# Two kinds of attention in one kernel: riding score units that may start later, and a new order from the 400th exponential on

## The chip, the core and the metric

The kernel runs on one core of a Trainium2 chip. The metric is the device time of one execution in microseconds (us), from its start to its last write. The core has a matrix engine (TensorE, PE in the profile), a vector engine (VectorE, DVE), an activation engine (ScalarE, ACT), a general engine (GpSimd, POOL) and a queue that issues most of the transfers (SyncE, SP). Matrix products land in PSUM, an accumulator memory whose banks hold 512 float32 columns on 128 partitions.

## The reference

One input x of 2048 tokens and 640 columns goes through two attentions with 32 heads of 20 columns each, and a gate mixes them:

```python
x = A_x
g = _sigmoid((x * gate_w).sum(-1, keepdims=True))
a = _A_ref(x, A_wqkv, A_wo)      # softmax over all 2048 keys
b = _B_ref(x, B_wqkv, B_wo)      # softmax over 8 keys: pos, pos-2, ..., pos-14
return g * a + (1 - g) * b
```

Attention A is the large part: 32 heads, 2048 queries and 2048 keys make 134 million exponentials. Attention B (window 8, step 2) is small in arithmetic, but has its own projections, and its elementwise products run on VectorE.

## The kernel before

**Groups, units, tiles.** Attention A is cut into 32 groups (GROUPS, L34): four heads times 512 queries. A group has 64 units: one head of the four, one block of 128 keys, 512 queries, so a unit is one score matmul with a 128x512 result. Two or three units make a tile; its scores lie side by side in PSUM, and one ACTIVATE with Exp on ScalarE (`exp`, L2000) turns a tile into bf16 in `ebuf`. Then matmuls (`pv`, L2045) multiply them with V and accumulate the whole group in one bank, `obank`. When a group is complete, `gen_norm` divides by the sums (which come out of the same matmuls, from a column of ones), multiplies by the gate and puts the result into `oTd`.

**Riding units.** A unit need not go through ScalarE. VectorE can make an approximation of the exponential: `clamp` (L1958) adds an offset to the scores and writes them as int16 into `uD`, whose bits are then read as bf16. Four such units, the four heads of one key block, make a quad. The quad enters the sum as four slices: `uD` itself and three copies with shifted exponents (`eD`), made either by one VectorE instruction for up to four units (`gen_d`, L1058) or in pieces of one unit on GpSimd (`piece`, L1089). Each slice has its own weight in V (`vS`, made on GpSimd, L1108). So a quad takes four units from ScalarE, and gives VectorE and GpSimd four clamps and three copies, and TensorE three slices of four matmuls more than the one set it would have had anyway. A riding unit's score matmul is issued together with a tile's ("rides" on it) into the third PSUM bank of the tile or another free one; so a tile that carries one has two units of its own as a rule.

**Banks.** Three PSUM banks serve everything else (BANKS: bank 0 is `sbank`, banks 1 and 2 are the last thirds of the two score buffers): projections, attention B, output blocks, riding units, and third units of tiles. In the profile, products into bank 0 are named side, those into 1 and 2 score.

**The planner.** Nothing of the order is written out by hand. While the program is built, a planner (`_Sched`) keeps an estimated time for each engine, emits tile after tile, and between them runs side jobs (Python generators with priorities: attention B in `gen_bproj` and `gen_b`, norms, output blocks in `gen_fold`, the riding copies in `gen_d`). The chip then executes each engine's fixed list, and semaphores keep the dependencies. Which job comes when depends on 22 numbers, and the table PLAN gives new ones at certain tile numbers:

```python
(SLACK, XTOL, XPRIO, XLATE, DWAIT, DIDLE, DIDLE2, DTIME, DLOW, DLATE, DVE_AHEAD, DAHEAD, BOOST, XBOOST, RFILL,
 FILL, HOLD, BOFF, EVS, FRT, PTAPS, PLATE) = plan
```

Among them are DTIME (a quad may be opened only while the exponentials still to come last at least that many us by the planner's clock, test in `wanted`), DIDLE and DIDLE2 (how idle VectorE must be for a ride), PTAPS (how many of attention B's products go to GpSimd), and the priorities of the side jobs.

**The end.** The last 512 tokens' output needs attention A and B of all heads. `gen_prefold` computes the parts that are ready earlier and stores them; `gen_prefold2` accumulates output blocks 2 and 3 in banks 0 and 1 and leaves them there for `tail`; before it takes the bank for block 3 it waits for `d_over`. `crowded` keeps bank 1 free of third units once no more than TLAST = 14 units of the last group are left. `tail` adds the last group's share after its norm (`gen_norm_last`, L950 to L969), and sends the rows out.

Of the kernel before, what the change touches and what calls it, by code (L numbers as in the profile page):

```python
# [423 lines left out]
def _build(ctx, nc, A_x, A_wqkv, A_wo, B_wqkv, B_wo, gate_w, out):  # L424
# [1480 lines left out]
    def d_over():  # L1905

        lo, hi = ahead[NG - 1]
        return cur["g"] >= NG - 1 and (4 * hi - lo) * UNIT < DTIME and not dopen
# [370 lines left out]
```

## Time and profile before

| | us |
|---|---|
| median of three runs | 775.98 (775.81 to 776.1) |
| the profiled execution, as a run | 776.33 |
| its span, from the first to the last instruction | 774.4 |
| first exponential of a tile starts | 18.0 |
| exponentials begun by 439.19 | 400 |
| last exponential ends | 766.41 |

The profile is of one execution. Its span leaves out what lies around the instructions, here 1.9 us. A row of a group gives the line, the engine, the operation, the tiles it writes and reads, the count, the union of the busy time and the mean duration of one, and the idle time of the engine before such instructions with what ended it. A row of a timeline gives the start, the length, and how many like instructions were merged. A row of windows gives the busy time of each engine in a stretch of the span. Instructions of one engine overlap at their ends in such records, so a sum of durations can exceed the union.

### The profile page before, as it was taken

To read this page: it belongs to the slowest core of one execution; us is meant where nothing else is said; L and a number is where in the kernel's file an instruction comes from. 1 tells how busy PE (TensorE), PEld (TensorE's weight loads), DVE (VectorE), ACT (ScalarE), POOL (GpSimd) and SP (SyncE) were. 2 spreads that over 40 slices of the span, in tenths; PEclk is the share of its full clock that TensorE was granted. 3 is DMA by queue.
4 is the path that set the end of the run, shared out by engine and by line. 5 is a ranking of instruction groups with operands and counts; after the bars stand their busy time and mean duration, and the time that the engine had idled before them with its cause. 6 is when DMAs were issued, how large, how long until landed. Compare 5 with 4: busy or idle time off the path is not lost.

```text
span 774.4 us, 30166 instructions
## 1 busy us (share of the span) xinstructions
PE 743.5 (96%) x12409; PEld 291.0 (38%) x12409; DVE 696.8 (90%) x1263; ACT 756.6 (98%) x747; POOL 353.8 (46%) x603
## 2 busy tenths in 40 slices
PE   8999999999998999999998999999999999999897
PEld 5433333332343343334334334433443423344233
DVE  6698978999999999979999999998999999998993
ACT  5999999999999999999999999999999999999996
POOL 4255633455753464344354445544453544253330
PEclk9999999999999999999999999999999999999999
DMA  7321122020111252331231122423204211133411
GB/s 232 113 64 38 31 61 60 26 47 14 40 36 36 54 130 67 80 98 52 74 95 45 24 57 61 96 65 91 49 27 110 52 27 49 46 71 82 109 31 37
DMA packets 71456, 49.89 MB, mean 64 GB/s; under 512 B 43096, under 2 KB 64872, under 8 KB 71320
## 3 DMA queue, kind: packets, MB, share of 16 engines
q1 hardware_dynamic: 70376, 47.54, 24.3%
q8 instruction: 99, 1.62, 0.9%
q10 hardware_dynamic: 944, 0.43, 0.2%
q14 instruction: 37, 0.30, 0.1%
HBM read 32.79 MB, written 7.62 MB: 52 GB/s over the span
## 4 chain that ended last, share of the span: by engine, by line
PE 45%; ACT 33%; issue 15%; DVE 6%; DMA 1%; SPq 0%; ACTq 0%; DVEq 0%
ACT ebuf L2000 33%; PE score L1981 14%; PE obank L2045 13%; PE side L691 11%; PE score L691 4%; DVE uD L1958 2%; DVE eD L1058 1%; DMA oB<-in_A_x_dram 1%; PE side L1239 1%; PE score L2066 0%; PE score L1685 0%; PE side L1347 0%; PE obank L2066 0%; DVE dst L841 0%; DVE kvw L1226 0%
## 5 line engine op out<-in xcount | busy, mean ns | idle before, releaser
L2000 ACT ACTIVATE ebuf<-score 128x1024 bf16<-128x1024 f32 (+1 forms) x706 | 743.2, 1198 | 3.0 <-PE score L1981 1.6
L1958 DVE TENSOR_SCALAR uD<-score 128x512 int16<-128x512 f32 x428 | 286.0, 681 | 30.0 <-PE score L1981 28.0
L1981 PE MATMUL score<-qT,kT 32*128 32x512 bf16 x1854 | 257.0, 384 | 16.5 <-ACT ebuf L2000 11.7
L1089 POOL TENSOR_TENSOR eD<-uD,two 128x256 int32<-128x256 int32 x311 | 186.7, 615 | 123.3 <-DVE eD L1058 59.3
L1058 DVE TENSOR_SCALAR eD<-uD 128x2048 int16<-128x2048 int16 (+3 forms) x295 | 173.6, 612 | 4.4 <-PE obank L2045 4.0
L2045 PE MATMUL obank<-ebuf,vA 128*21 128x512 bf16 x1616 | 152.7, 385 | 0.9 <-ACT ebuf L2000 0.7
L1981 PEld LDWEIGHTS score<-qT,kT 32*128 32x128 bf16 x1854 | 63.7, 91 | 211.4 <-ACT ebuf L2000 148.3
L1108 POOL TENSOR_TENSOR vS<-vA,vw 128x252 bf16<-128x252 bf16 x108 | 65.4, 606 | 111.7 <-DVE eD L1058 66.0
L2045 PE MATMUL obank<-eD,vS 128*21 128x512 bf16 x1296 | 110.7, 379 | 0.0
L691 PE MATMUL side<-xT,wBs 128*32 128x256 bf16 x2400 | 95.6, 281 | 0.7 <-DVE rQ L1301 0.5
L691 PEld LDWEIGHTS side<-xT,wBs 128*32 128x32 bf16 x2400 | 68.3, 141 | 28.6 <-issue 16.3
L1031 POOL TENSOR_TENSOR oN<-oTt,oN 128x256 bf16<-128x256 f32 x60 | 47.5, 791 | 58.7 <-DVE eD L1058 29.3
L2045 PEld LDWEIGHTS obank<-ebuf,vA 128*21 128x21 bf16 x1616 | 36.7, 89 | 82.8 <-issue 60.3
L1164 DVE CAST qkvB<-side 128x512 bf16<-128x512 f32 (+1 forms) x72 | 42.1, 594 | 3.9 <-PE side L691 3.6
L1335 DVE TENSOR_TENSOR kvw<-kvw,eB 128x2048 bf16<-128x2048 bf16 (+1 forms) x40 | 44.5, 1138 | 0.0
L1226 DVE TENSOR_TENSOR kvw<-qkvB 128x1792 bf16<-128x1792 bf16 (+2 forms) x40 | 44.4, 1133 | 0.1
L2045 PE MATMUL obank<-uD,vA 128*21 128x512 bf16 x432 | 41.9, 379 | 0.0
L2045 PEld LDWEIGHTS obank<-eD,vS 128*21 128x21 bf16 x1296 | 31.5, 91 | 19.6 <-issue 2.0
L1016 POOL TENSOR_TENSOR rcp<-rcp,gA 128x16 f32<-128x16 f32 x30 | 7.8, 259 | 56.2 <-DVE rcp L1012 26.8
L1981 PE MATMUL score<-woBp,kT 32*128 32x512 bf16 x188 | 30.0, 384 | 1.7 <-ACT ebuf L2000 0.9
L691 PE MATMUL side<-xT,kvw 128*32 128x512 bf16 (+1 forms) x340 | 28.6, 383 | 0.5 <-DVE vA L917 0.2
L691 PE MATMUL side<-kvw,xT 128*32 128x160 bf16 (+1 forms) x760 | 28.5, 262 | 0.5
(212 smaller groups left out, 575.5 us busy)
## 6 DMA issues: line engine op xcount, KB each, us to landing
kvw<-scr_v SPq DMA_DIRECT2D x32, 336.5 KB
oN<-scr_n SPq DMA_DIRECT2D x60, 128.0 KB
scr_v<-qkvB SPq DMA_DIRECT2D x32, 85.0 KB
wBs<-in_B_wqkv_dram SPq DMA_DIRECT2D x5, 480.0 KB
WqP<-in_A_wqkv_dram SPq DMA_DIRECT2D x14, 160.0 KB
oTd<-oN SPq DMA_DIRECT2D x108, 20.0 KB
out_dram<-outsb SPq DMA_DIRECT2D x12, 160.0 KB
qT<-dst SPq DMA_DIRECT2D x93, 20.0 KB
```

The lines of the kernel that those rows point to most:

```text
L691: ins = e.matmul(o[j:k, :], l(j) if callable(l) else l[:, j:k], r, start=(first and i == 0), stop=(last and i == n - 1), skip_group_check= ...
L1031: T("pool", 0.73, lambda e, cols=cols: e.tensor_tensor(oN[0][:, cols], oTt[:, cols], rcpR[:, cols], ALU.mult), reads=["oTt", "oN%d" % i], ...
L1058: T("dve", 0.065 + 0.1334 * (n - m), lambda e, k=k, sl=sl, m=m: e.tensor_scalar(eD[:, sl % NS, 512 * m:512 * n].bitcast(I16), uD[d % 2][:, ...
L1089: T("pool", PDUR, lambda e: e.tensor_tensor(eD[:, sl % NS, 512 * i:512 * (i + 1)].bitcast(I32), uD[d % 2][:, 512 * i:512 * (i + 1)].bitcas ...
L1108: T("pool", 0.607, lambda e: e.tensor_tensor(vS[:, d % 2, :, :], _ap(vA, (kb * NQ + q) * 4 * DV, [[0, K - 1], [1, 4 * DV]]), _ap(vw, 0, [[ ...
L1164: t = TB(dvc(n * TOK), lambda e, o=o, i=i: e.tensor_copy(o, i), reads=[("side", b)], writes=[key])
L1226: TB(dvc(n_ * TOK, 2), lambda e: e.tensor_tensor(o, i0, i1, ALU.mult), reads=["qB", "kB"], writes=prods(i, range(n_)) + olds(), port=True)
L1335: TB(dvc(n_ * 2 * TOK, 2), lambda e: e.tensor_tensor(o, i0, i1, ALU.mult), reads=rd, writes=prods(i, range(2 * n_)), port=True)
L1958: t = T("dve", 0.598, lambda e: e.tensor_scalar(uD[d % 2][:, 512 * i:512 * (i + 1)].bitcast(I16), side[x], UOFF, 0.0, op0=ALU.add, op1=ALU ...
L1981: ins = e.matmul(o, kT[32 * j:32 * j + 32, q, kb * P:(kb + 1) * P], qT[qbuf[g]][32 * j:32 * j + 32, :], start=True, stop=True)
L2000: exps[s] = T("act", actc(512 * n), lambda e: e.activation(ebuf[s % NE][:, 0:512 * n], score[s % 2][:, 0:512 * n], ACTF.Exp, scale=LN2 / S ...
L2045: ins = e.matmul(obank[32 * j:32 * j + DV, :], v, src, start=(kb == 0), stop=(last and k >= len(lst) - 4), skip_group_check=True)
```

## The change

One predicate and the table change. In the predicate, block 3's bank is no longer tied to DTIME: it may be taken when the units left in the last group, with the open quad's, are at most 14. The table's rows up to tile 395 and those of tiles 425 and 590 stay; the others from 400 on are new, so all that is emitted after the 400th exponential can come in another order. DTIME is the eighth number of a row. No instruction of a new kind is added.

```diff
-    400: ((0.34, 0.55), 0.4, 1, 1.0, 0.75, -1.26, -0.12, 7.8, 1.29, 9.17, 0.97, 0.39, 6.33, 4.29, 0.03, 0.59, 2, -2.27, 0.3, -1.0, (2, 2), 0.2),
-    405: ((0.34, 0.55), 0.4, 1, 2.06, 0.75, -1.26, -0.12, 7.8, 1.29, 9.17, 0.97, 0.39, 6.33, 4.29, 0.03, 0.59, 2, -2.27, 0.3, -1.0, (2, 2), 0.2),
...
-    640: ((0.369, 0.753), 0.25, 1, 2.69, 1.07, -0.99, -0.43, 13.26, 1.53, 9.17, 0.86, 0.47, 4.85, 3.41, 0.1, 0.68, 2, -7, 0.17, -1.0, (1, 0), 0.27),
...
-    695: ((0.369, 0.753), 0.41, 1, 3.21, 0.75, -1.48, -0.92, 13.26, 1.53, 6.0, 0.86, 0.47, 4.56, 2.94, 0.1, 0.62, 2, -6, 0.3, -1.0, (1, 0), 0.2),
-    705: ((0.565, 0.745), 0.41, 1, 3.21, 0.75, -1.48, -0.92, 13.26, 1.53, 6.0, 0.86, 0.47, 4.56, 2.94, 0.1, 0.62, 2, -6, 0.3, 0.0, (1, 0), 0.18),
+    400: ((0.34, 0.55), 0.4, 1, 1.0, 0.75, -1.26, -0.12, 7.8, 1.29, 9.17, 0.97, 0.39, 6.33, 4.29, 0.03, 0.59, 2, -2.27, 0.3, -1.0, (2, 2), 0.11),
+    405: ((0.34, 0.55), 0.4, 1, 1.0, 0.75, -1.26, -0.12, 7.8, 1.29, 9.17, 0.97, 0.39, 6.33, 4.29, 0.03, 0.59, 2, -2.27, 0.3, -1.0, (1, 2), 0.11),
...
+    675: ((0.503, 0.796), 0.27, 2.61, 3.21, 1.15, -1.48, -0.92, 13.26, 4.7, 6.39, 0.92, 0.32, 4.63, 1.83, 0.1, 0.64, 2, -6, 0.49, -1.0, (1, 0), 0.2),
+    680: ((0.503, 0.796), 0.4, 2.61, 1.0, 0.89, -1.26, -0.92, 7.8, 7.0, 6.39, 0.91, 0.3, 4.63, 4.07, 0.08, 0.64, 2, -6, 0.3, -1.0, (1, 0), 0.2),
...
+    705: ((0.508, 0.701), 0.4, 2.47, 3.63, 0.79, -1.26, 0.05, 7.8, 1.53, 6.7, 0.83, 0.32, 4.63, 4.07, 0.13, 0.66, 2, -5.33, 0.3, -1.0, (1, 0), 0.2),
 }
...
     def d_over():

         lo, hi = ahead[NG - 1]
-        return cur["g"] >= NG - 1 and (4 * hi - lo) * UNIT < DTIME and not dopen
+        return cur["g"] >= NG - 1 and 4 * hi - lo + len(dopen) <= TLAST
```

98 rows, old and new, of the table PLAN are left out of this document.

## The prediction

> **What bounds the kernel now.** I read the page first: the busy row, the slices, and the chain that ended last.
>
> ```profile
> span 774.4 us, 30166 instructions
> ...
> PE 743.5 (96%) x12409; PEld 291.0 (38%) x12409; DVE 696.8 (90%) x1263; ACT 756.6 (98%) x747; POOL 353.8 (46%) x603
> ...
> DVE  6698978999999999979999999998999999998993
> ACT  5999999999999999999999999999999999999996
> ...
> PE 45%; ACT 33%; issue 15%; DVE 6%; DMA 1%; SPq 0%; ACTq 0%; DVEq 0%
> ```
>
> ScalarE is full in every slice but the first and the last, TensorE and VectorE are nearly so, GpSimd is half empty. Busy time alone doesn't say which of three full engines sets the pace, so I read who waits for whom:
>
> ```profile
> ACT ebuf L2000 <- PE score L1981: 1.6, 5, 0.5
> ...
> PEld score L1981 <- ACT ebuf L2000: 164.5, 419, 1.2
> ```
>
> Exponentials waited for scores 1.6 us in all; scores waited for exponentials 164.5 us, because a tile's PSUM comes free only when its exponential ends. So ScalarE sets the pace and TensorE follows. Now the part that the change can touch, from where 400 exponentials have begun: the exponentials by form, and VectorE's load.
>
> ```profile
> 0.00:439.19 439.19, 418.56 (x400) 1.00 0.26 66
> ```
>
> ```profile
> L2000 ACT ACTIVATE ebuf<-score 128x1024 bf16<-128x1024 f32 x212 | 204.1, 1071 | 1.1 <-PE score L1981 0.6
> L2000 ACT ACTIVATE ebuf<-score 128x1536 bf16<-128x1536 f32 x94 | 133.3, 1500 | 0.0
> ...
> L2000 ACT ACTIVATE ebuf<-score 128x512 bf16<-128x512 f32 x1 | 0.6, 605 | 0.0
> ```
> ```profile
> 439.00:756.00 317.00, 292.50 (x493) 1.00 0.26 63
> 756.00:766.40 10.40, 1.95 (x4) 1.00 0.01 3
> ```
>
> The last two rows are VectorE's busy time. From 439 to 766.4 ScalarE does 212 double, 94 triple and one single unit: 424 + 282 + 1 = 707 units, the row at 439 included. The span of 327.4 us over 707 is 0.463 us for a unit. VectorE has 317.0 - 292.5 = 24.5 us idle up to 756 and 8.45 us between 756 and 766.4.
>
> The last 19 us are different, and the timeline shows it:
>
> ```profile
> 737.90 28.51 ACT L2000 ACTIVATE ebuf<-score 128x1024 bf16<-128x1024 f32 x25
> 745.02 0.67 DVE L1958 TENSOR_SCALAR uD<-score 128x512 int16<-128x512 f32 x1
> 755.64 0.43 DVE L1372 SCALAR_TENSOR_TENSOR oB<-side,rB 128x256 bf16<-128x256 f32 x1 [0.56 <-PE side L1347]
> 755.98 1.28 DVE L1058 TENSOR_SCALAR eD<-uD 128x2048 int16<-128x2048 int16 x2
> 756.12 0.46 PE L691 MATMUL side<-woBp,oB 128*32 128x128 bf16 x20 [0.21 <-DVE oB L1372]
> ...
> 760.41 0.40 PE L691 MATMUL side<-woBp,oB 128*32 128x512 bf16 x4
> 764.10 0.39 PE L691 MATMUL score<-woBp,oB 128*32 128x512 bf16 x4
> ...
> 767.13 0.78 DVE L950 STREAM_TRANSPOSE oTt<-obank 128x256 f32<-128x256 f32 x2 [6.78 <-PE obank L2045]
> 769.12 0.10 PEld L1464 LDWEIGHTS side<-outsb,oN 128*32 128x32 bf16 x4 [0.37 <-DVE oN L969]
> ```
>
> The last ride is at 745.0. Attention B's last eviction (L1372) ends at 756.07, and from there TensorE has a run of output products: the stored part of the last block from 756.12, block 2 into bank 0 from 760.41, block 3 into bank 1 from 764.10. The last exponential ends at 766.41 (737.90 + 28.51), then the last norm runs on VectorE from 767.13, and TensorE waits only 0.37 us for it at 769.12. So two chains reach 769.12 nearly together: ScalarE's with the norm, and TensorE's output products behind B's last eviction, with 0.37 us of slack.
>
> **The change part by part.** The test in `d_over`: block 3 took its bank at about 764, 2.3 us before the last exponential, when by 0.463 us per unit some five units were left. The old bound (13.26 us) and the new one (14 units, 6.5 us) both lay behind it by then; block 3 followed block 2, and block 2 followed the eviction. Alone, the line moves nothing here: cost 0, and if a quad were open at 764 it lets block 3 go up to its end earlier than before, a matter of one ride, 0.7 us.
>
> DTIME falls from 13.26 to 7.8 for the last tiles. Counted back from 766.4, quads could be opened until about 753.2, and now until 758.6. VectorE is busy until 757.26 (755.98 + 1.28), then nearly idle: so the new stretch has room for one quad. That is the first quad I count.
>
> The new table from tile 400 on can place more quads in VectorE's 24.5 idle us. What a quad costs there comes from the whole run's groups:
>
> ```profile
> L1958 DVE TENSOR_SCALAR uD<-score 128x512 int16<-128x512 f32 x428 | 286.0, 681 | 30.0 <-PE score L1981 28.0
> L1089 POOL TENSOR_TENSOR eD<-uD,two 128x256 int32<-128x256 int32 x311 | 186.7, 615 | 123.3 <-DVE eD L1058 59.3
> L1058 DVE TENSOR_SCALAR eD<-uD 128x2048 int16<-128x2048 int16 (+3 forms) x295 | 173.6, 612 | 4.4 <-PE obank L2045 4.0
> ```
> ```profile
> L1958 DVE TENSOR_SCALAR uD<-score 128x512 int16<-128x512 f32 x179 | 119.5, 681 | 13.2 <-PE score L1981 12.4
> L1058 DVE TENSOR_SCALAR eD<-uD 128x2048 int16<-128x2048 int16 x81 | 54.5, 691 | 3.4 <-PE obank L2045 3.4
> ```
>
> In the whole run the 428 clamps (some records may be missing) are 107 quads: (286.0 + 173.6) / 107 = 4.30 us of VectorE and 311 / 107 = 2.9 pieces of 0.615 us on GpSimd for each. 24.5 / 4.30 = 5.7 quads would fit at most, with no gap left; none if the gaps are too short to use (by the last fence, the same from 439 to 756, 13.2 of those us stand before clamps that wait for their scores). Neither end is likely. I take one more quad, since an idle share of 24.5 / 317 = 8% lies in pieces, of which a reordering gathers a fifth: 4.3 us. So two quads, eight units off ScalarE.
>
> A unit off a triple tile saves 1500 - 1071 = 429 ns, and 0.463 us is the upper price above. Eight units: -3.43 us (to -3.70).
>
> What they cost TensorE: three slices more for each quad, and the rows give a slice:
>
> ```profile
> 757.45 0.40 PE L2045 MATMUL obank<-ebuf,vA 128*21 128x512 bf16 x4
> 757.67 0.60 PE L2045 MATMUL obank<-eD,vS 128*21 128x512 bf16 x8
> ```
>
> A set of four starts 0.22 us before the next (757.45 to 757.67), so a quad adds 0.66 us. Ahead of 740 that hides in TensorE's waits for exponentials. In the tail it stands in the run of output products: 0.66 - 0.37 of slack = +0.29 us, for the one quad there.
>
> For the whole gain to arrive, that run must also start 3.4 us earlier, so B's last unit has to be done at 752.6 in place of 756.07. There is cover: between 740 and 756 TensorE spends this much on filler (L2066, products that nobody reads).
>
> ```profile
> 740.00:756.00 16.00, 3.28 (x48) 1.27 (x48) 1.00 0.09 25
> ```
>
> The first number after the length is TensorE's busy time on L2066: 3.28 us can go. On VectorE, B's products compete with the quads; that cost is the last rival.
>
> One more term: an order never run may add waits of exponentials for scores. This run has 1.6 us of them over 706 tiles; the 306 new ones could have none more, or as much again as all of this run. I take 0.5 us.
>
> The Trainium skill (Perfetto Trace Analysis, Identifying the Most-Contended Engine) says that matmul busy time is a poor measure of how near TensorE is to its limit, and that weight-load time is a better one. By it TensorE, at 38%, has room, the slices in the tail cost nothing, and the sum would be 0.29 us lower. Here the trace disagrees for the tail alone: the wait of 0.37 us at 769.12 says that little room is left there, and I keep the term.
>
> **The sum.** 776.33 (the profiled execution) - 3.43 + 0.29 + 0.5 = 773.69. The runs' median lies 0.35 below the profiled execution, so 773.3 us.
>
> **The rivals.**
>
> *More than that* (four or five quads). For it: GpSimd is 46% busy, and the new rows give other shares of B's products to it, which frees VectorE. Against it: GpSimd waited 59.3 us for VectorE's copies (the L1089 row), so it isn't free when it looks idle. Four to five quads are 16 to 20 units, 6.9 to 8.6 us, less the same 0.8: 768.2 to 769.9. Three lie between, at 771.6. The Trainium skill (SBUF — State Buffer, Who interferes with whom) says that VectorE in its two-port modes and GpSimd lock each other out of a shared port for a whole instruction. The 59.3 us agree with it; by it copies driven off GpSimd fall on VectorE, a quad then costs an estimated 4 x 0.681 + 3 x 0.691 = 4.80 us there, and five quads would take 24.0 of the 24.5 idle us.
>
> *Nothing measurable.* The rule didn't bind at 764, and the order from 400 on was full already: ScalarE has no gap to close, 8% of VectorE's time in small pieces may hold no quad, and the tail's quad may replace an earlier one. Then 707 units stay 707, and the time is 775.98 with up to 0.79 us of the costs above: 776.0 to 776.8.
>
> *Slower: the tail hangs on B's last unit.* A new order that puts rides ahead of B's products delays B's last eviction. Behind it stands TensorE's run from 756.12 to 769.12 with 0.37 us of slack, so each us of delay beyond that is a us at the end, however early the exponentials finish. One quad's work on VectorE ahead of it is 4.30 us: +3.9, 779.9 us. A delay of half of that, 2.15 us, gives +1.8, 777.8. It decides from about 0.4 us of delay on. For it: the new rows keep low priorities for B in many rows and open quads later; against it: the same VectorE is free from 757, so a late quad needn't go ahead of B.
>
> That the order changes nothing at all is not a case: 306 tiles follow new numbers.
>
> **How the numbers follow.** What a measurement of this kernel can tell from no change is about 0.2%, 1.55 us: faster means below 774.4, slower above 777.5. Forecast with one to three quads: 0.50, own range 771.6 (three) to 775.0 (one: 775.98 - 1.72 + 0.79), of which 0.06 lies above 774.4. Four or more: 0.13. Nothing: 0.15. Slower: 0.22. So faster 0.44 + 0.13 = 0.57, same 0.06 + 0.15 = 0.21, slower 0.22. The range takes in most of the larger gain, down to 769.8, and the milder half of the slower case, up to 778.2; it leaves out some 0.06 below and 0.12 above.
>
> **What the changed profile would show.** If I am right: fewer units in the L2000 rows after 439 (699, or 1612 in the whole run), 436 clamps or so, a ride after 753, B's last eviction before 754, the last exponential near 763, and still 8 us from there to the end. Wrong by the slower case: the last eviction of L1372 is as late as before or later, ScalarE ends early and the wait at L1464 is gone, with VectorE idle for longer ahead of L950. Nothing: 707 units again. The forecast also falls if the waits of L2000 for L1981 grow by more than 2 us, or if the 8 us from the last exponential to the end become longer.

## The result, and the profile after

| | before | after |
|---|---|---|
| median of seven runs each, us | 775.98 | 778.29 |
| ratio, with its 95% interval | | 1.0031 (1.002 to 1.0043) |
| profiled execution, span, us | 774.4 | 776.2 |
| exponentials (tiles) of the run | 706 | 707 |
| 400 begun, the 401st starts, us | 439.20 | 438.84 |
| from there to the end of the last, us | 327.21 | 327.06 |
| from there to the end of the span, us | 8.0 | 10.3 |

The changed kernel is slower by 0.3%. The three last rows add up to the difference of the spans: -0.36 before anything that changed, -0.15 in the tiles from the 401st on (306 before, 307 after), +2.3 behind the last exponential, 1.8 us. From the page of the changed kernel:

```profile
span 776.2 us, 30204 instructions
...
PE 745.9 (96%) x12412; PEld 292.1 (38%) x12413; DVE 704.2 (91%) x1276; ACT 754.0 (97%) x748; POOL 357.1 (46%) x610
...
PE 49%; ACT 29%; issue 12%; DVE 8%; DMA 1%; SPq 0%; ACTq 0%; DVEq 0%
...
L1962 DVE TENSOR_SCALAR uD<-score 128x512 int16<-128x512 f32 x436 | 292.4, 684 | 29.5 <-PE score L1985 27.6
```

The line numbers of this kernel are four higher (L2004 for L2000 and so on). ScalarE is busy 2.6 us less and VectorE 7.4 us more, the chain that ended last has moved from ScalarE to TensorE by four points, and the clamps are eight more: two quads. ScalarE's exponentials from there on, by form, then its waits over the whole run, and VectorE's load:

```profile
L2004 ACT ACTIVATE ebuf<-score 128x1024 bf16<-128x1024 f32 x223 | 214.7, 1080 | 2.8 <-PE score L1985 2.5
L2004 ACT ACTIVATE ebuf<-score 128x1536 bf16<-128x1536 f32 x84 | 119.4, 1506 | 0.4
L2004 ACT ACTIVATE ebuf<-score 128x512 bf16<-128x512 f32 x1 | 0.6, 597 | 0.0
```
```profile
ACT ebuf L2004 <- PE score L1985: 3.5, 10, 0.8
```
```profile
439.00:756.00 317.00, 296.28 (x501) 1.00 0.26 63
756.00:766.40 10.40, 5.47 (x9) 1.00 0.01 3
```

446 + 252 + 1 = 699 units where there were 707, and the three rows' busy time is 334.7 us where it was 338.0: 3.3 us less work, nearly the 8 times 0.429 = 3.43 of the forecast. But the idle time ahead of them is 2.8 + 0.4 = 3.2 us where it was 1.1, and the waits for scores in the whole run are 3.5 us in ten places where they were 1.6 in five. VectorE's idle time up to 756 went from 24.5 to 20.7 us.

The last 20 us, from timelines of the changed kernel:

```profile
746.45 19.45 ACT L2004 ACTIVATE ebuf<-score 128x1024 bf16<-128x1024 f32 x17 [0.77 <-PE score L1985]
759.75 0.42 DVE L1376 SCALAR_TENSOR_TENSOR oB<-side,rB 128x256 bf16<-128x256 f32 x1
760.39 0.45 PE L695 MATMUL score<-woBp,oB 128*32 128x128 bf16 x20
764.12 0.39 PE L695 MATMUL side<-woBp,oB 128*32 128x512 bf16 x4
766.40 0.78 DVE L954 STREAM_TRANSPOSE oTt<-obank 128x256 f32<-128x256 f32 x2 [1.36 <-PE obank L2049]
768.01 0.31 DVE L973 STREAM_TRANSPOSE oN<-oN 128x128 f32<-128x128 f32 x1
768.70 0.31 DVE L973 STREAM_TRANSPOSE oN<-oN 128x128 f32<-128x128 f32 x1
770.94 0.39 PE L1468 MATMUL side<-outsb,oN 128*32 128x512 bf16 x4
```

The last norm is ready earlier than before: its two transposes (0.31 us each) now end at 768.32 and 769.01, where they were at 769.06 and 769.74. Yet its products start at 770.94, and the wait of 0.37 us that stood at that row is gone: TensorE comes 2.6 us after the first of the transposes and 1.9 us after the second, where before it waited for both. B's last eviction ends at 760.17 in place of 756.07. How TensorE's work is split around the last exponential, in windows of the two kernels that begin with the end of that eviction and break at the end of the last exponential (columns: length, then the busy time of PE, PEld, DVE, ACT and POOL, each with its count, then granted clock, DMA share and GB/s), first before, then after:

```profile
756.06:766.41 10.35, 10.29 (x239) 4.44 (x239) 1.89 (x4) 10.35 (x10) 0.00 (x0) 1.00 0.01 3
766.41:774.40 7.99, 4.12 (x112) 1.92 (x104) 4.53 (x14) 1.08 (x2) 0.00 (x0) 1.00 0.25 85
```
```profile
760.17:765.90 5.73, 5.73 (x181) 3.04 (x173) 1.30 (x3) 5.59 (x6) 0.00 (x0) 1.00 0.03 6
765.90:776.20 10.30, 6.30 (x152) 3.23 (x148) 4.49 (x14) 1.08 (x2) 0.00 (x0) 1.00 0.19 66
```

Ten exponentials ended behind the eviction, now six. The output products that TensorE did beside the four others now stand behind the last one: 4.12 us of TensorE became 6.30, +2.18 of the +2.3 at the end.

### The profile page after: what moved, and what is told of

Its sections match the earlier page's. It is cut to its first block, busy times and chain, and to the rows that moved or that the text cites. A ratio compares the mean times of both kernels' runs of the same rounds, so it can differ in the third digit from the quotient of the medians.

```text
span 776.2 us, 30204 instructions
## 1 busy us (share of the span) xinstructions
PE 745.9 (96%) x12412; PEld 292.1 (38%) x12413; DVE 704.2 (91%) x1276; ACT 754.0 (97%) x748; POOL 357.1 (46%) x610
## 4 chain that ended last, share of the span: by engine, by line
PE 49%; ACT 29%; issue 12%; DVE 8%; DMA 1%; SPq 0%; ACTq 0%; DVEq 0%
ACT ebuf L2004 28%; PE score L1985 16%; PE obank L2049 14%; PE side L695 11%; PE score L695 5%; DVE uD L1962 3%; DVE eD L1062 1%; DMA oB<-in_A_x_dram 1%; DVE kvw L1230 1%; PE side L1351 1%; PE side L1243 1%; DVE kvw L1339 1%; PE score L2070 0%; PE obank L2070 0%; PE score L1689 0%
## 5 line engine op out<-in xcount | busy, mean ns | idle before, releaser
L2004 ACT ACTIVATE ebuf<-score 128x1024 bf16<-128x1024 f32 (+1 forms) x707 | 740.3, 1195 | 5.1 <-PE score L1985 3.5
L1962 DVE TENSOR_SCALAR uD<-score 128x512 int16<-128x512 f32 x436 | 292.4, 684 | 29.5 <-PE score L1985 27.6
L1062 DVE TENSOR_SCALAR eD<-uD 128x2048 int16<-128x2048 int16 (+3 forms) x300 | 177.2, 614 | 2.6 <-PE obank L2049 2.2
L1035 POOL TENSOR_TENSOR oN<-oTt,oN 128x256 bf16<-128x256 f32 x60 | 45.8, 763 | 49.7 <-DVE eD L1062 32.1
L1221 POOL TENSOR_TENSOR kvw<-qkvB 128x256 bf16<-128x256 bf16 x38 | 22.9, 612 | 22.6 <-DVE kvw L1230 7.0
```

What stands on the lines that cost most here:

```text
L1035: T("pool", 0.73, lambda e, cols=cols: e.tensor_tensor(oN[0][:, cols], oTt[:, cols], rcpR[:, cols], ALU.mult), reads=["oTt", "oN%d" % i], ...
L1062: T("dve", 0.065 + 0.1334 * (n - m), lambda e, k=k, sl=sl, m=m: e.tensor_scalar(eD[:, sl % NS, 512 * m:512 * n].bitcast(I16), uD[d % 2][:, ...
L1962: t = T("dve", 0.598, lambda e: e.tensor_scalar(uD[d % 2][:, 512 * i:512 * (i + 1)].bitcast(I16), side[x], UOFF, 0.0, op0=ALU.add, op1=ALU ...
L2004: exps[s] = T("act", actc(512 * n), lambda e: e.activation(ebuf[s % NE][:, 0:512 * n], score[s % 2][:, 0:512 * n], ACTF.Exp, scale=LN2 / S ...
```

## The experiments

Times are medians, beside the kernel before on the same chip. With the new predicate in `d_over` alone, the kernel before is built into the same five lists of instructions in the same order; and the changed kernel keeps its own lists with the old predicate and DTIME at 13.26 from row 680 on. So neither the predicate nor the smaller DTIME at the end does anything here: the other numbers of the table make the whole difference.

### A late quad alone

```diff
-    690: (..., -0.99, -0.43, 13.26, 1.53, ...),   (and 695, 705)
+    690: (..., -0.99, -0.43, 7.8, 1.53, ...),
```

> The kernel before with DTIME 7.8 in its last rows (tiles 690 on) and nothing else: the order stays the same up to about 750 us, then one more quad rides, 109 in place of 108. By the prediction's step (a quad in the idle VectorE of the tail): four units off ScalarE, 4 x 0.429 = 1.72 us, less 0.29 us of TensorE: 1.4 us faster, 774.6 us. By the tail theory (the end is set by TensorE's output products behind attention B's last eviction): the last exponential is 1.2 to 1.7 us earlier, but the quad adds three slices of 0.22 us to TensorE and nothing brings the eviction forward, so the end is 0.66 - 0.37 = 0.3 us later or a little more, 776.3 to 776.8 us, and TensorE's wait for the last norm (0.37 us before) is gone.

Measured: 776.88 beside 775.89 us, ratio 1.0011 (1.0002 to 1.002). One quad more, in the empty tail as my first term had it: three of its four clamps stand behind B's last eviction. The timeline:

```profile
757.63 0.68 DVE L1958 TENSOR_SCALAR uD<-score 128x512 int16<-128x512 f32 x1
765.41 0.78 DVE L950 STREAM_TRANSPOSE oTt<-obank 128x256 f32<-128x256 f32 x2 [2.77 <-PE obank L2045]
767.72 0.31 DVE L969 STREAM_TRANSPOSE oN<-oN 128x128 f32<-128x128 f32 x1
769.30 0.39 PE L1464 MATMUL side<-outsb,oN 128*32 128x512 bf16 x4
```

The last ride ends at 758.3 and the norm is ready at 768.03, but TensorE gets to it at 769.30, without a wait. The last exponential does come 1.2 us earlier (326.00 us after the 401st in place of 327.21), but the eviction doesn't (316.84 us in place of 316.86), and TensorE has the slices to do on top. ScalarE's gain isn't collected at the end; the slices cost. So a quad in the idle tail is a loss of about 1 us (0.2 to 1.6 by the interval), and not a gain of 1.4. That is a little more than the 0.3 us or so of the tail theory, and what the rest is stays open.

### TensorE's work behind the last exponential, taken away and added

```diff
-  ... mm_group(b, fold_mms(..., blk, qs, 0, 512, True, range(FE)), rd, mmc(512), last=False)
+  ... mm_group(b, fold_mms(..., blk, qs, 0, 512, True, range(FE)), rd, mmc(512), last=False, skip=range(7 * (blk == 3)))
-  ... [...] + WQ, mmc(512), first=False, last=False)
+  ... [...] + WQ, mmc(512), first=False, last=False, skip=range(blk == 3))
```

In the changed kernel:

> The changed kernel in the same order, with 8 of the 10 product sets of the last output block's first 512 columns left out (5 of attention B, 3 of A; the rows of that block are then not the reference's). In its trace they stand behind the last exponential, 767.3 to 769.6 us, 0.215 us each. Tail theory: 8 x 0.215 = 1.72 us less, 776.6 us, the last exponential where it was. Rival (the waits of exponentials for scores, earlier in the kernel, made it slower): no change, 778.3 us.

In the kernel before:

> The kernel before with the same 8 product sets left out. There TensorE waits 0.37 us for the last norm, which follows the last exponential. Tail theory with two chains that tie: no gain, 776.0 us (775.8 to 776.1), and TensorE's wait for the norm grows from 0.37 to 1 us or more. Rival (every product in the tail counts, in either kernel): 1.72 us less, 774.3 us.

And the other way round in the kernel before:

```diff
-            mm(("half", blk), first(half(blk), blk, q, 0, 512), False, rl, [("score", 0)][blk:])
+            mm(("half", blk), first(half(blk), blk, q, 0, 512) * 3, False, rl, [("score", 0)][blk:])
```

> The kernel before with 8 product sets more (the last group's products into blocks 0 and 1 done three times; those rows are then not the reference's) between the last exponential and the last norm's products. Tail theory: 8 x 0.215 = 1.72 us, of which the wait of 0.37 us swallows its part: 1.35 us slower, 777.3 us. Rival (ScalarE and the norm alone set the end before): no change, 776.0 us.

Measured, beside 775.89: 776.45 for the first (1.0009, 1.0 to 1.0018), 776.40 for the second (1.0005, 0.9996 to 1.0013), 777.25 for the third (1.0019, 1.001 to 1.0028). TensorE's arrival at the last norm in the three; for the second, also where it waits for the last exponential:

```profile
770.00 0.39 PE L1468 MATMUL side<-outsb,oN 128*32 128x512 bf16 x4
```
```profile
766.68 0.61 PE L2045 MATMUL obank<-ebuf,vA 128*21 128x512 bf16 x8 [1.02 <-ACT ebuf L2000]
```
```profile
769.33 0.10 PEld L1464 LDWEIGHTS side<-outsb,oN 128*32 128x32 bf16 x4 [0.79 <-DVE oN L969]
```
```profile
769.88 0.39 PE L1464 MATMUL side<-outsb,oN 128*32 128x512 bf16 x4
```

In the changed kernel it comes 3.31 us after the last exponential (766.69) in place of 5.04, so eight sets are worth 1.73 us and the time falls by nearly as much. In the kernel before the same omission only lengthens waits: the one for the norm from 0.37 to 0.79 us (I had expected 1 us or more), and a new one of 1.02 us for the last exponential takes most of the rest. Eight sets added there cost 1.36 us, which is 1.73 less the slack of 0.37. So the changed kernel's end hangs on TensorE, the end of before on the norm, and the slack is what the prediction read.

### TensorE and VectorE where both are full

The exponentials wait longer from 670 us on. Up to the last exponential ScalarE is idle there for 0.52 us before and 2.56 us after (ACT is the fourth busy time), most of the 2.4 us that it is idle longer in all:

```profile
670.00:766.41 96.41, 90.37 (x1645) 37.65 (x1637) 80.22 (x130) 95.89 (x90) 32.01 (x56) 1.00 0.27 64
```
```profile
670.00:765.90 95.90, 91.67 (x1625) 36.27 (x1617) 83.86 (x132) 93.34 (x91) 30.05 (x51) 1.00 0.26 64
```

In the changed kernel B's last two units do all of their elementwise products there (from 670.88 us on, the last unit from 725.55), and from 725 to 742 us both engines are full: TensorE is busy for 16.47 of 17.00 us and VectorE for 16.80, where they were for 14.42 and 14.57 before. Three runs left work out of this stretch.

```diff
-  ... fold_mms(side[b][:, :], i, qs, 0, 512, True, range(FE)), rd, mmc(512))
+  ... fold_mms(side[b][:, :], i, qs, 0, 512, True, range(FE)), rd, mmc(512), skip=range(1, 7))
```

> The changed kernel in the same order, with 12 of the 16 product sets of the last output rows' first two stored blocks left out (those rows are then not the reference's). They stand at 725 to 735 us of its trace, 12 x 0.215 = 2.6 us of TensorE, in a stretch where TensorE is busy 16.47 of 17.00 us. If TensorE is what the exponentials wait for there: the waits of exponentials 672 to 690 go, the last exponential comes at least 1 us earlier counted from the 400th, and the end with it, 777.3 us or less. If it is VectorE: no change, 778.3 us.

```diff
-                o = _ap(stage, i * CH, [[TOK, n_], [1, TOK]])
+                o = _ap(stage, i * CH, [[TOK, n_ if u < 7 else 1], [1, TOK]])
...
```

> The changed kernel in the same order, with attention B's first five products of its last unit made for one of seven taps only (VectorE reads and writes a seventh; that unit's rows are then not the reference's). They stand at 725 to 733 us, some 1.1 us each, of which about 0.9 goes: 4.5 us of VectorE, in a stretch where VectorE is busy 16.80 of 17.00 us. If VectorE is what the exponentials wait for there (late clamps, late banks): the last exponential comes at least 1 us earlier counted from the 400th, the end with it, 777.3 us or less. If it is TensorE: no change, 778.3 us.

Both together:

> The changed kernel in the same order with both omissions of the last two runs. If the two full engines share the blame, neither run alone brings the whole of the waits back and this one does: the last exponential some 2 us earlier counted from the 400th, 776.3 us. If one of them has it alone, this run is no faster than that one's. If the waits come from the fixed order alone (a product set behind an eviction that is late for another reason), all three stay at 778.3 us.

Measured: 779.65 (1.005, 1.0037 to 1.0062), 778.24 (1.0032, 1.0021 to 1.0044) and 777.09 (1.0013, 1.0004 to 1.0022). The first was slower, and its windows say why: the last column but two is the granted clock. Below them, the first two windows of the run with both omissions.

```profile
725.00:728.00 3.00, 2.17 (x27) 0.59 (x19) 3.00 (x5) 3.00 (x4) 0.67 (x2) 1.00 0.16 35
728.00:731.00 3.00, 2.66 (x35) 0.98 (x39) 2.95 (x5) 2.63 (x4) 0.98 (x2) 0.88 0.55 147
731.00:734.00 3.00, 2.64 (x19) 0.41 (x11) 3.00 (x5) 2.52 (x3) 0.73 (x1) 0.50 1.06 209
734.00:737.00 3.00, 3.00 (x24) 0.59 (x21) 1.91 (x4) 2.29 (x3) 1.52 (x3) 0.50 0.40 88
```
```profile
725.00:728.00 3.00, 2.36 (x24) 0.64 (x20) 1.49 (x6) 3.00 (x5) 1.23 (x2) 1.00 0.19 45
728.00:731.00 3.00, 2.60 (x40) 0.93 (x36) 2.67 (x5) 3.00 (x5) 0.73 (x1) 1.00 0.67 167
```

The clock of a TensorE with less to do went down to half for some 6 us, and ScalarE ran dry. In the run with both omissions, which leaves out the same 12 product sets, the clock stayed at 1.00. So the first run tells nothing of a full TensorE, and its omission was made once more at a smaller size, in the second of the two blocks alone:

```diff
+  ... rd, mmc(512), skip=range(1, 7 if i else 1))
```

> The changed kernel in its own order, but of the second stored output block (the stretch from about 731 to 735 us) six of eight product sets are left out; the first one keeps all of its products, so that TensorE has no long light stretch. Six sets at 0.215 us (1.72 us for eight in the second run) are 1.3 us of TensorE. Theory, that a full TensorE by itself held the exponentials back there: granted clock 1.00 in every window from 725 to 742, first 400 exponentials to the last exponential 326.0 (327.06 in the changed kernel), time 777.0 to 777.4. Rival, that it takes the load of both engines: 326.7 to 327.1 and 777.9 to 778.4. If the clock falls again (under 0.95 in a window), the run says nothing on either, and the time is above 778.5.

Measured: 777.65 beside 776.26 (1.0018, 1.0009 to 1.0027), clock 1.00 throughout. From the start of the 401st to the end of the last exponential: 327.06 us in the changed kernel, 326.66 with less on VectorE, 326.43 with less on TensorE, 325.80 with both (there twelve sets on TensorE). These are single traces; the run with eight sets less behind the last exponential, which has the changed kernel's work up to there, has 326.93, so 0.1 us is no difference. The one block brought 0.63 us, half of the 1.3 that a full TensorE by itself would have to give back. So the load of TensorE holds some 0.6 us, that of VectorE 0.4, both together 1.3 of the time that was lost; neither is the whole of it. Of the first 0.4 us nothing is seen in the time (778.24).

### B's last unit made light

Six sets of the second block as above, and the ten products of B's last unit on VectorE cut to their first part:

```diff
-                o = _ap(stage, i * CH, [[TOK, 2], [2 * TOK, n_], [1, TOK]])
+                o = _ap(stage, i * CH, [[TOK, 2], [2 * TOK, n_ if u < 7 else 1], [1, TOK]])
...
```

> The changed kernel in its own order, with the same six sets left out, and of attention B's last unit the ten products on VectorE cut short: five at L1230 on one of their seven taps, five at L1339 on a quarter of their columns. By the rows (1.124 to 0.388 us each, and 1.221 to about 0.45) VectorE is spared 7.5 us, of which 3.8 stand behind 751. Theory, that the last unit of B loses the gain twice, by waits of exponentials while it competes with the rides, and by TensorE's run behind its last eviction: last eviction near 757.0 or before (760.17), eight or more exponentials to end behind it, the wait of TensorE for the last norm at L1468 back, last exponential 764.4 to 764.9, time 775.0 to 776.0. Rival, that B's last unit isn't what costs: time 777.0 or more, with the eviction earlier or not.

> The kernel before in its own order, with the same three things left out of it. Its waits of exponentials after 670 us are 2.7 us against 5.4 in the changed kernel, and its last norm sets the end already but for 0.37 us. Theory: little to gain, 775.0 to 775.7, and the pair with both last units light differs by less than the 2.3 us that the two kernels differ by, the changed one perhaps ahead by up to 1 us. If the two quads brought their whole 3.4 us wherever B's last unit doesn't stand in the way, the changed one would be ahead by 2.5 us or more. Rival, that the changed order loses elsewhere: it stays 2 us behind this run.

Measured: 777.25 (1.0018, 1.0009 to 1.0027) and 776.06 (0.9999, 0.9991 to 1.0008), beside 776.26. The first fell short of the theory, 775.0 to 776.0 with eight or more exponentials behind the eviction; the second gained nothing, less than the little I had given it. The eviction of the first, and the count of exponentials from there to the last (second number in brackets), then the same two rows of the kernel before made light:

```profile
757.57 0.42 DVE L1376 SCALAR_TENSOR_TENSOR oB<-side,rB 128x256 bf16<-128x256 f32 x1 [0.67 <-PE side L1351]
...
757.99:764.22 6.23, 6.23 (x6) 1.00 0.02 5
```
```profile
755.54 0.42 DVE L1372 SCALAR_TENSOR_TENSOR oB<-side,rB 128x256 bf16<-128x256 f32 x1 [1.36 <-PE side L1347]
...
755.97:766.37 10.40, 10.40 (x10) 1.00 0.01 3
```

Six and ten again. VectorE now stands idle ahead of the eviction, waiting for TensorE's sums of B's products, and these stand in TensorE's list between the scores of certain tiles. The list is worked off in its order, and scores wait for exponentials; so the eviction comes after the same exponential however fast VectorE is. The other runs bear it out: in all nine traces with the changed kernel's list six exponentials end behind the eviction, wherever it falls between 757.99 and 761.52 us, and in all four with the list of before ten. That was the flaw in my theory for this pair: B's lateness isn't a race that VectorE loses at the end; it is written into the order. The pair still differs by 1.2 us with both last units light. At the last exponential the changed kernel is then ahead by 1.3 us, counted from the 401st (325.94 and 327.27 us), and it loses 2.7 behind it: TensorE reaches the last norm 5.04 us after the last exponential, as in the changed kernel.

### The filler ahead of a wait

```diff
-        def fn(e):
+        def fn(e, n_=8 if 686 <= len(exps) < 691 else 512):
...
-   ins = e.matmul(o[...], ..., xT[:, 0, 1536:2048], start=bool(best),
+   ins = e.matmul(o[..., :n_], ..., xT[:, 0, 1536:1536 + n_], start=bool(best),
```

> The changed kernel in its own order; six sets of L2070 between 741.0 and 744.9 us (products that nobody reads) are 8 columns wide in place of 512. Nothing of the output changes. In the changed kernel the exponential at 746.45 waits 0.77 us for scores that start at 746.01; ahead of them stand, from 743.95, two sets of L2070 (0.43 us), a 0.23 us wait for a clamp's bank, and six sets of slices (1.3 us) in TensorE's list. Theory, that these waits come from the place in TensorE's list: the scores start up to 0.4 us earlier against the exponential before, the wait falls from 0.77 to 0.3 to 0.5 us, and the last exponential, the last eviction and the end follow by as much: 777.8 to 778.1. Rival, that VectorE's clamps hold it: the wait stays at 0.7 to 0.8 us and the time at 778.2 to 778.4. If the granted clock falls, a time above 778.5.

The second with `len(exps) >= 655`:

> The changed kernel in its own order; all 27 sets of L2070 after 670 us are 8 columns wide in place of 512. Nothing of the output changes. Most of them stand where TensorE waits for an exponential anyway, so they give no more than the run before: 777.6 to 778.1, with six exponentials still to end behind B's last eviction and the norm's wait at L1468 gone as in the changed kernel. Rival, that TensorE's total load delays B's last sums: then the eviction moves ahead of one or more exponentials (seven or eight behind it) and the time falls below 777.4. If the granted clock falls under 0.95 in a window after 670, a time above 778.5.

Measured: 778.58 (1.0036, 1.002 to 1.0052) and 779.51 (1.0042, 1.0026 to 1.0059) beside 775.96; neither gained what was expected, and in both six exponentials end behind the eviction. In the first the wait stayed, as the rival had it, but not for the rival's reason, and the theory had the wrong part of TensorE's list. The timeline of the first:

```profile
743.80 2.01 ACT L2004 ACTIVATE ebuf<-score 128x1024 bf16<-128x1024 f32 x2
...
744.95 0.61 PE L2049 MATMUL obank<-ebuf,vA 128*21 128x512 bf16 x8 [0.49 <-ACT ebuf L2004]
...
745.39 0.39 PE L2049 MATMUL obank<-uD,vA 128*21 128x512 bf16 x4
...
745.60 0.60 PE L2049 MATMUL obank<-eD,vS 128*21 128x512 bf16 x8
...
746.14 0.39 PE L1985 MATMUL score<-qT,kT 32*128 32x512 bf16 x3
...
746.58 1.02 ACT L2004 ACTIVATE ebuf<-score 128x1024 bf16<-128x1024 f32 x1 [0.76 <-PE score L1985]
```

TensorE had time to spare: it waits 0.49 us for the exponential that ends at about 744.8. Released by it, it first does five sets of products (20 matmuls, 1.2 us; I had counted six) and only then the scores that ScalarE needs at 745.81, where its second exponential ends. So the wait of 0.76 us is read as one of order: slices ahead of scores, both free from the same moment. No run with the scores ahead was made. In the changed kernel and all eight experiments with its order it stood there at 0.76 us or more.

In the second run the clock fell again, in the windows that follow a TensorE emptied of filler:

```profile
744.00:746.00 2.00, 1.53 (x20) 0.53 (x20) 1.93 (x7) 1.33 (x2) 0.00 (x0) 0.71 0.20 33
746.00:748.00 2.00, 2.00 (x18) 0.31 (x10) 1.18 (x2) 0.97 (x1) 0.99 (x2) 0.50 0.10 25
```
```profile
747.03 2.10 ACT L2004 ACTIVATE ebuf<-score 128x1024 bf16<-128x1024 f32 x2 [1.70 <-PE score L1985]
```

## Why the prediction was wrong

Forecast were 773.3 us and faster; measured were 778.29 and slower, 0.1 us above the range. By its own steps:

- **The predicate costs and moves nothing**: right, shown by the unchanged lists of instructions.
- **Two quads, eight units, 0.429 us each**: right. 699 units, 436 clamps, and 3.3 us less work on ScalarE. (In the whole run there are 1608 units and not the 1612 of the forecast: four more clamps in each kernel read bank 0 and stand in a row of their own, so the quads went from 108 to 110.)
- **Where the quads come from**: wrong. The quad that I put into VectorE's empty tail wasn't placed there: the last clamp ends at 750.7, and the smaller DTIME changes no instruction. Had it been, the first experiment shows what it brings: not 1.72 - 0.29 = 1.4 us, but a loss of 1. There ScalarE's gain and TensorE's cost are not two terms of one sum, since TensorE's chain sets the end once its slack of 0.37 us is used.

```profile
750.00 0.69 DVE L1962 TENSOR_SCALAR uD<-score 128x512 int16<-128x512 f32 x1 [0.17 <-PE score L1985]
```

- **"For the whole gain to arrive, that run must also start 3.4 us earlier, so B's last unit has to be done at 752.6 in place of 756.07. There is cover"**: this is the step that failed. I named the condition and then took it as met, because TensorE had 3.28 us of filler there. The eviction came 4.1 us later instead of 3.4 earlier, and the cost that the sum had at nothing was +2.3 us behind the last exponential. The cover wasn't taken either: the new order has more filler in the same stretch, 4.70 us in place of 3.28.

```profile
740.00:756.00 16.00, 4.70 (x64) 1.32 (x64) 1.00 0.20 49
```

Nor is filler room for B: it stands where TensorE waits for exponentials. With six sets of it cut short and the clock at 1.00 the eviction came 0.3 us earlier, counted from the 401st exponential (321.06 us in place of 321.33), for some 1.3 us of TensorE, and stayed behind the same exponential. What sets it is its place in TensorE's list.

- **0.5 us for waits of a new order**: mis-sized. ScalarE's windows from the 401st exponential to the last, before and after (ACT is the fourth busy time):

```profile
439.20:766.41 327.21, 316.00 (x5456) 125.58 (x5448) 294.26 (x495) 326.10 (x319) 139.95 (x242) 1.00 0.25 61
```
```profile
438.84:765.90 327.06, 315.66 (x5416) 124.62 (x5408) 301.91 (x508) 323.55 (x320) 144.53 (x249) 1.00 0.25 61
```

Idle time went from 1.11 to 3.51 us, +2.4, and busy time fell by 2.55. That is 0.75 less than the 3.3 of the three rows, whose records overlap each other where exponentials follow without a wait. So the units were gone and the time was not: 2.4 - 2.55 = -0.15 us.

- **The slower rival**: its mechanism is the one that came, with two of the signs named for it (late eviction, the wait at L1464 gone). The other two didn't: ScalarE ended only 0.5 us earlier, and VectorE's idle time ahead of the last norm is 1.36 us in place of 6.78. Its price was too high: 3.9 us for 4.30 us of delay, where the delay of 4.1 cost 1.8 in the span. From the eviction to the end it took 18.4 us before and takes 16.1 now, because the scores and products of four exponentials are no longer behind it (TensorE's busy time from the eviction to the end is 12.0 us in place of 14.4). A later eviction pushes other work ahead of itself.
- **GpSimd's 59.3 us**: the prediction set them beside a shared port, and they don't show one. `piece` issues each of GpSimd's copies with `after=last_port()`, so the program itself makes GpSimd wait for VectorE's last copy or product; what a port would do without that, no run here shows.
- **The "nothing" rival** would have read the pace rightly (0.15 us gained), for another reason than it gave: the order wasn't too full to hold more quads.

Why B's last unit has a later place can be followed back. Windows of B's evictions alone (L1372, L1376 after, three to a unit) show that it fell behind by 590 us: six of them lie between 439 and 590 before, and five after.

```profile
439.00:590.00 151.00, 3.57 (x6) 1.00 0.26 64
```
```profile
439.00:590.00 151.00, 2.74 (x5) 1.00 0.25 61
```

B then made up most of it: the last eviction of the third unit from the end comes 17.1 us later than before (at 670.96 us), of the last but one 5.5 (725.63), of the last 4.1. That the added rides there took VectorE's time from B's products (35 clamps lie between 550 and 600 us where 29 did), and that the new table's other priority for B in rows 525 to 550 (-3 in place of -6 to -7) let them, is argued and not tried. Open too is the rest of the lost gain, about 1 us, that neither the load of both engines (1.3) nor the one late score (0.76) explains. No order that beats both kernels was run.

## What to carry to other kernels

When a full engine is relieved, look at what the other engine still has to do after it: the gain arrives only if that work moves ahead by as much, and here which exponential it comes after was set by its place in an in-order list, not by how busy the engines were. Count what remains of each engine's work behind the last instruction of the bounding one; here 4.12 us became 6.30 and decided the sign. A condition that the sum needs ("must also start 3.4 us earlier") is a term with a price of its own, not a remark.

## What the runs showed of the hardware

Taking work from TensorE was followed twice by a lower granted clock. With 12 product sets left out, its busy share from 725 to 728 us was 2.17 of 3 us, and the granted clock went to 0.88, then 0.50 for two windows of 3 us; with the filler cut short after 670 us it went to 0.71 and 0.50 in windows of 2 us, and the wait of one exponential grew from 0.77 to 1.70 us. From the 401st to the last exponential these two runs took 328.08 and 328.22 us, where the changed kernel took 327.06 with more to do. Their times, 1.005 and 1.0042 of the kernel before beside 1.0031, have intervals that overlap with its own. The Trainium skill (TensorE: Matmul & The Clock Gate, Part 1: The HAM clock gate) has the clock at half rate after an idle window. The 0.50 agrees; but in these windows TensorE wasn't idle, only some three quarters busy. The busy share of such a window alone doesn't decide it either: with the same 12 sets left out and less on VectorE the clock stayed at 1.00 at 2.36 and 2.60 of 3 us, and in the run with six sets of filler cut short it stayed at 1.00 at 1.15 and 1.51 of 2 us:

```profile
742.00:744.00 2.00, 1.15 (x26) 0.61 (x26) 1.13 (x2) 2.00 (x4) 0.61 (x1) 1.00 0.26 41
744.00:746.00 2.00, 1.51 (x31) 0.55 (x31) 2.00 (x6) 1.82 (x2) 0.00 (x0) 1.00 0.20 33
```

It isn't fixed by the program: the six executions with all of the filler cut short have mean clocks from 0.992 (780.71 us) to 1.000 (777.57 us).
